# An adaLN attention and Mish block on one core: constants by memset, joint modulation visits, early weight preparation, and another order and pace of the dense work before the first exponential

## The chip, the cores and the metric

The kernel runs on one core of a Trainium2 chip. The metric is the device time of one execution in microseconds; the median of three runs stands for a kernel. Engines: PE is TensorE, DVE VectorE, ACT ScalarE, POOL GpSimd, SP SyncE, which issues every DMA of this kernel.

## The reference

All inputs are float32; x has 2048 rows of 512, there are 32 heads of 16, and F is 1792.

```python
mod = (_silu(c) @ w_mod).reshape(c.shape[0], 6, 1, -1)
sa, ca, ga, sb, cb, gb = (mod[:, i] for i in range(6))
h = _layernorm(x) * (1 + ca) + sa
x = x + ga * (softmax(q @ k.T * Dh ** -0.5) @ v) @ wo      # q, k, v = h @ wqkv
h = _layernorm(x) * (1 + cb) + sb
x = x + gb * (mish(h @ w1 + b1) @ w2)
```

## The kernel before

**Steps.** Attention is cut into 32 iterations n (four blocks of 512 queries by eight groups of four heads). An iteration has 16 steps, one for each 128 keys, and 512 steps t in all, with 20 more (t = -20 to -1) ahead of them. In each step PE makes four products for the softmax maxima of an iteration that lies 20 steps ahead (`max_pair` L493 before t = 0, `max_tile` L479 after it), which DVE reduces (L503, L489); four score products (`score`, L532, L536), whose exponential ACT takes (L539); and the product of older exponentials with the values (`pv`, L554). A step is two half steps; the schedule is written by hand in half steps h = 2t, 2t+1: `at(h, f)` hangs f on a half step, and `run_hooks` runs it there. All instructions of an engine run in the order in which they were emitted, and all DMAs are issued by SP in that order too and share one hardware queue.

**Dense work.** Everything else for PE (the projections to q, k and v, the output projection, the MLP) is cut into units of mostly twelve matmuls of 512 columns, taken in the order of one list when their ready time has come. In steps before t = 0 `whole_units` (L1204) takes as much as a credit allows, `CREDIT` = 7.5 columns blocks of 512 for each step, and the last matmul may run over; a value unit has matmuls of 256 columns, which count one half. From t = 2 on `next_part` (L1185) lays up to eight slots over two steps, one 64-row half in each, beside the score and maximum products. `plan` (L1337) lists the projections: value half 0, keys 1 (`(1, 1)`), queries 1 (`(0, 1)`), keys 2, queries 2, and so on. The end of unit i splits the weights of unit group i+2 into a high and a low part (`slice_split`, ACT and POOL) and loads those of i+3 (`slice_load`). Results go to DRAM scratch, and `load_pair` (L321) brings keys and queries of two heads back into one of NR = 5 buffers `ka`, `qa`. Rows 48 to 63 and 112 to 127 of these hold constants: ones in `ka`, zeros in `qa`, two of them overwritten by minus the maxima (`max_rows` L514, put by four DMAs `qa<-mt`, L525, six half steps ahead of the iteration). The constants come by DMA (`zeros`, `one`, and copies of `ka[0]` for the last three buffers).

**Modulation.** Four vectors of the modulation are made while attention runs: each of eight halves is loaded (`mod_load` L645), summed on POOL, and visited by PE (`mod_unit` L658) as a special between the score products and `pv`; two halves are in flight.

**Preparation.** 32 slices of w1, wo and w2 are then loaded, split on POOL into high and low, and stored to DRAM scratch (`prep_unit` L678, paced by `start_preps` L1392): a new load waits, in half steps, for the store that last used its buffer. `store_at` and `load_at` keep some half steps of an iteration free. When all are stored and the projections done, `open_mlp` gives their space to the MLP, and `first_loads` (L822) loads the first weights of `block(0, 272)`. A block (output projection, transposes, up and down products of one query block) fills 128 steps.

Of the kernel before, what the change touches and what calls it, by code (L numbers as in the profile page):

```python
# [8 lines left out]
F32 = mybir.dt.float32  # L9
F32R = mybir.dt.float32r  # L10
# [8 lines left out]
def adaln_block(ctx: ExitStack, tc: tile.TileContext, x, wqkv, wo, w1, b1, w2, c, w_mod, out):  # L19
# [20 lines left out]
    CUT1, CUT2 = (0, 1), (2, 3)  # L40
    LOV = ((1,), (), (1, 3), (1, 3))
    PREP = 4
    CREDIT = 7.5
    HCAP = 10.0

    x = x[0]
# [77 lines left out]
    def mm(acc, l, r, start, stop):  # L124
        pe_queue.append((acc, l, r, start, stop))
# [71 lines left out]

    def load_at(h):

        return h if h < 60 or 2 <= h % 32 < 20 else h - h % 32 + 28 if 20 <= h % 32 <= 28 else h + -(h - 2) % 32  # L200

    def at(h, f):

# [122 lines left out]
    with ExitStack() as es:  # L326
# [83 lines left out]
        stats_tb(1)  # L410
        tr_tb(0)
        apply_tb(1)
        def zeros(i):
            for b in (48, 112):
                nc.sync.dma_start(qa[i][b:b + 16, :].bitcast(F32), zer[:16, :])

        for i in range(2):
            for b in (48, 112):
                nc.sync.dma_start(ka[i][b:b + 16, :].bitcast(F32), one[:64, :])
            zeros(i)  # L420

        def constants():
            for i in range(2, NR):
                zeros(i)
            for q4 in range(S // TB):
                nc.sync.dma_start(dap(qscr, 48 * S + q4 * TB, [[50 * S, H], [S, 2], [1, TB]]), zer[:64, :])
            nc.sync.dma_start(dap(vscr, VROW - 16, [[VROW, P], [P * VROW, G], [1, 16]]), zer[:, :16 * G])
            nc.sync.dma_start(b1c, b1.rearrange("(f p) -> p f", p=P))
# [226 lines left out]
            mst["row at", i] = h + 7  # L655
        at(h + 7, sums)

    def mod_unit(i):  # L658

        v, o = divmod(i, 2)  # L660
        gate = v in (2, 5)
        acc, row = ring(), mst.pop(("wm", i))[:, 0]
        if gate:
            mm(acc[:, :2 * P], ones.to_broadcast([P, P]), row, True, True)
        else:
            for m in range(2):
                mm(acc[:, m:m + 1], row[:, m * P:(m + 1) * P], ones, True, True)

        def fin(h):
            if gate:  # L670
                nc.scalar.copy(gates[(v - 2) // 3][:, o * 2 * P:(o + 1) * 2 * P], acc[:, :2 * P])
            elif v == 4:
                nc.vector.tensor_scalar_add(modc[:, v - 1, 2 * o:2 * o + 2], acc[:, :2], 1.0)
            else:
                nc.vector.tensor_copy(modc[:, v - 1, 2 * o:2 * o + 2], acc[:, :2])
        return fin

    def prep_unit(h, third, scr, src, gate):  # L678
# [113 lines left out]
    def block(qb, t0):  # L792
# [389 lines left out]
    def queue_special(ready, make):  # L1182
        specials.append((ready, make))
# [146 lines left out]
    def do_specials(h):  # L1330
        if specials and h >= specials[0][0]():
# [27 lines left out]
        return fin  # L1359

    at(-2 * PRO, lambda: slice_load(*plan[2][1:3]))
    order = (4, 5, 10, 11, 6, 7, 8, 9)

    def first_mods(h):
        for i in order[:2]:
            mod_load(i, h)

    def queue_mod(j):
        def make():
            put = mod_unit(order[j])  # L1370

            def fin(h):
                put(h)
                if j + 2 < len(order):
                    mod_load(order[j + 2], h)
                elif j + 1 == len(order):
                    start_preps(h + 2)
            return fin

        queue_special(lambda: mst.get(("row at", order[j]), 4 * T) + 6, make)  # L1380

    for j in range(len(order)):
        queue_mod(j)
    for i, (t0, _, _, args) in enumerate(plan):
        for a in args:
            queue(lambda i=i, t=t0: max(2 * t, split_at.get(i, 4 * T) + 4), lambda tag, i=i, a=a: planned(i, a, tag))

    preps = [(w1scr[f], w1[:, f * P:(f + 1) * P].rearrange("(k p) m -> p k m", p=P), None) for f in range(FT)]
    preps += [(woscr[k], wo[k * P:(k + 1) * P, :], 0) for k in range(DK)]
    preps += [(w2scr[f], w2[f * P:(f + 1) * P, :], 1) for f in range(FT)]  # L1390

    def start_preps(h, i=0, turn=0, puts=()):  # L1392

        if i == len(preps):
            mst["open"] = (max(puts) + 2) // 2
            return
        three = (2, 1, NKC - 1) in put_away
        prep_unit(h, three and turn % 3 == 2, *preps[i])
        puts = (*puts, store_at(h + 9))[-3 if three else -2:]
        then = load_at(max(h + PREP, puts[0] + 1 if len(puts) > 2 - (not three) else 0))  # L1400
        at(then, lambda: start_preps(then, i + 1, turn + 1 if three else 0, puts))

    def prep_step(t):
# [19 lines left out]
    at(2 * (T - 28), lambda: load_ys((0, 1)))  # L1423
    at(2 * (T - 12), lambda: load_ys((2,)))
    at(2 * T - 30, tail_loads)
    for pp in range(2, NR):
        for b in (48, 112):
# [43 lines left out]
```

## Time and profile before

| | before |
|---|---|
| runs | 1700.04, 1703.48, 1704.23 us; median 1703.48 |
| profiled execution | 1704.48 us, its span 1702.7 us, granted clock 0.996 |
| busy | PE 98%, DVE 84%, ACT 80%, POOL 48% of the span |
| DMA | 240.08 MB, 49.5% of 16 engines' span |
| start to the first step (0 to 50.15 us) | layernorm and first projections |
| steps before t = 0 (50.15 to 102.95 us) | maxima of iteration 0 and a part of 1, dense work |
| steps from t = 0 | to about 1600 us |
| last query block's MLP | from there to the end |

Times in the profile count from the span's start. PE's busy time counts overlapping matmuls once and takes in time in which they wait for operands, so a full row does not say that PE does all it can; the pace of the steps, from one `pv` to the next, says more.

### The profile page before, as it was taken

Reading aid. Unit: us, or ns where it says so; the run is one execution under the profiler, and the core shown is the slowest. Engines: PE = TensorE matmul, PEld = TensorE weight load, DVE = VectorE, ACT = ScalarE, POOL = GpSimd, SP = SyncE. Lnnn points to the kernel's source line nnn. Section 1 sums busy time; section 2 is a strip of 40 time slices with the busy share of each in tenths; the row PEclk is TensorE's granted clock in tenths of the full one; section 3 lists DMA queues with packets and bytes.
Section 4 is the critical chain, followed back from the end, with each engine's and each line's share of the span. In section 5 each row is a group of like instructions: output and inputs, shape, how many; then the busy total and the mean of one; then the engine's idle time right before and its main releaser. Section 6 shows DMA issues by size and latency. Waiting matters only on the chain.

```text
span 1702.7 us, 33730 instructions
## 1 busy us (share of the span) xinstructions
PE 1674.4 (98%) x12406; PEld 921.7 (54%) x12406; DVE 1438.2 (84%) x2372; ACT 1359.4 (80%) x2614; POOL 809.3 (48%) x829
## 2 busy tenths in 40 slices
PE   7999999999999999999999999999999999999999
PEld 5755665455444545555555455555555455555587
DVE  6888888888889898888889898888889888884377
ACT  6257777777778998888888998888888988888674
POOL 5155224565513465645433464655323564555442
PEclk9999999999999999999999999999999999999999
DMA  7777467777773343425364434435354433433261
GB/s 252 186 233 216 111 163 214 238 229 217 236 219 94 89 105 90 128 78 135 80 161 122 129 73 109 124 76 139 78 141 134 130 93 76 142 105 127 78 229 62
DMA packets 113997, 240.08 MB, mean 141 GB/s; under 512 B 24048, under 2 KB 49648, under 8 KB 107784
## 3 DMA queue, kind: packets, MB, share of 16 engines
q1 hardware_dynamic: 113832, 237.92, 49.5%
q8 instruction: 98, 1.61, 0.4%
q14 instruction: 67, 0.55, 0.1%
HBM read 179.95 MB, written 51.44 MB: 136 GB/s over the span
## 4 chain that ended last, share of the span: by engine, by line
PE 90%; DVE 3%; DMA 3%; ACT 2%; issue 1%; SPq 0%; POOL 0%; ACTq 0%; DVEq 0%; POOLq 0%
PE bk L554 28%; PE ring L536 22%; PE ring L487 19%; PE bk L136 10%; PE bk L129 3%; PE ring L1162 2%; PE ring L129 2%; DVE mx L489 2%; ACT pr L539 1%; DMA qa<-mt 1%; DMA xt<-in_A_x 1%; PE ring L501 1%; DMA w<-w1scr 1%; DMA w<-woscr 1%; PE ring L865 0%
## 5 line engine op out<-in xcount | busy, mean ns | idle before, releaser
L489 DVE TENSOR_REDUCE mx<-ring 128x1 f32<-128x512 f32 x1968 | 1222.9, 682 | 159.5 <-PE ring L487 138.0
L539 ACT ACTIVATE pr<-ring 128x512 f32<-128x512 f32 x2048 | 1079.0, 602 | 216.2 <-PE bk L136 118.0
L487 PE MATMUL ring<-ka,qa 64*128 64x512 f32 x1968 | 819.0, 429 | 3.0 <-DMA od<-ot 1.3
L536 PE MATMUL ring<-qa,ka 64*128 64x512 f32 x2048 | 761.3, 403 | 6.8 <-DMA qa<-mt 4.0
L554 PE MATMUL bk<-pr,vg 128*32 128x512 f32 x4096 | 546.8, 606 | 0.0
L487 PEld LDWEIGHTS ring<-ka,qa 64*128 64x128 f32 x1968 | 350.8, 184 | 331.6 <-DVE mx L489 248.1
L536 PEld LDWEIGHTS ring<-qa,ka 64*128 64x128 f32 x2048 | 374.1, 184 | 201.5 <-DVE mx L489 114.0
L136 PE MATMUL bk<-h,w 64*128 64x512 f32 (+1 forms) x1080 | 279.0, 391 | 0.0
L136 PE MATMUL bk<-w,a_h 64*128 64x512 f32 x632 | 210.6, 413 | 0.0
L136 PEld LDWEIGHTS bk<-h,w 64*128 64x128 f32 x1080 | 178.3, 184 | 9.6 <-ACT pr L539 1.5
L554 PEld LDWEIGHTS bk<-pr,vg 128*32 128x32 f32 x4096 | 80.8, 108 | 136.9 <-issue 127.8
L136 PE MATMUL bk<-w,a_l 64*128 64x512 f32 x316 | 124.2, 393 | 0.0
L136 PEld LDWEIGHTS bk<-w,a_h 64*128 64x128 f32 x632 | 106.9, 184 | 2.6
L921 POOL TENSOR_TENSOR y<-yd,y 128x512 f32<-128x512 f32 x44 | 56.9, 1293 | 89.5 <-ACT yd L920 84.6
L756 POOL TENSOR_SCALAR qq<-ee 128x512 f32<-128x512 f32 x25 | 15.5, 622 | 169.1 <-ACT ee L750 169.1
L772 POOL TENSOR_TENSOR qq<-qq,rr 128x512 f32<-128x512 f32 x42 | 54.2, 1291 | 83.6 <-ACT rr L766 83.4
L758 POOL TENSOR_TENSOR hb<-hb,ee 128x512 f32<-128x512 f32 x42 | 54.1, 1289 | 82.4 <-DVE ee L754 80.4
L136 PE MATMUL bk<-w,o_hl 64*128 64x512 f32 x288 | 79.8, 407 | 0.0
L98 POOL TENSOR_TENSOR a_l<-hb,a_h 128x512 fp32r<-128x512 f32 x53 | 72.2, 1363 | 4.4
L136 PEld LDWEIGHTS bk<-w,a_l 64*128 64x128 f32 x316 | 58.3, 184 | 2.3
L136 PE MATMUL bk<-h_h,wl 64*128 64x512 f32 x168 | 57.5, 423 | 0.0
L774 POOL TENSOR_TENSOR rr<-rr,qq 128x512 f32<-128x512 f32 x42 | 54.1, 1289 | 3.5
(206 smaller groups left out, 1857.9 us busy)
## 6 DMA issues: line engine op xcount, KB each, us to landing
ka<-kscr SPq DMA_DIRECT2D x124, 384.0 KB
w<-w2scr SPq DMA_DIRECT2D x56, 512.0 KB
w<-w1scr SPq DMA_DIRECT2D x46, 512.0 KB
vg<-vscr SPq DMA_DIRECT2D x32, 552.0 KB
qa<-qscr SPq DMA_DIRECT2D x124, 100.0 KB
kscr<-qh SPq DMA_DIRECT2D x16, 512.0 KB
qscr<-qh SPq DMA_DIRECT2D x32, 256.0 KB
hl<-in_B_w SPq DMA_DIRECT2D x28, 256.0 KB
```

The costliest lines, as they stand in the source:

```text
L98: (nc.gpsimd if eng == "p" else nc.vector).tensor_sub(lo, src, hi.bitcast(F32))
L129: nc.tensor.matmul(acc, l, r, start=start, stop=stop)
L136: i = nc.tensor.matmul(acc, l[64 * g:64 * g + 64], r[64 * g:64 * g + 64], start=start and not then, stop=bool(stop and then))
L487: nc.tensor.matmul(pm, qt[64 * s:64 * s + 64, qs * P:(qs + 1) * P], kt[64 * s:64 * s + 64, kb * TB:(kb + 1) * TB], start=True, stop=True)
L489: nc.vector.tensor_reduce(out=mxs[n][:, s, 4 * j + qs, kb:kb + 1], in_=pm, op=ALU.max, axis=AX.X)
L536: nc.tensor.matmul(p_, kt[64 * s:64 * s + 64, kc * P:(kc + 1) * P], qt[64 * s:64 * s + 64, :], start=True, stop=True)
L539: e = nc.scalar.activation(pr, p_, AF.Exp, scale=SCALE)
L554: nc.tensor.matmul(accs[n][32 * h:32 * h + 32, :], vgs[n][:, o:o + 32], pts.pop((t, h)), start=(kc == 0), stop=(kc == 15))
L758: (nc.vector if tail else nc.gpsimd).tensor_mul(hb, hb, ee)
L772: nc.gpsimd.tensor_mul(qq, qq, rr)
L774: nc.gpsimd.tensor_mul(rr, rr, qq)
L921: nc.gpsimd.tensor_add(y[i], yd, y[i])
```

## The change

It has these parts, in the order of the code:

- `CREDIT` is 7.4, and `whole_units` keeps in `cur["owed"]` what a step took too much or too little.
- The constant rows of `qa` and `ka` come from POOL memsets of whole tiles, three of 128x2048 for `ka[2:]` after the setup; 20 small DMAs go.
- In `plan` queries 1 stand ahead of keys 1, so their weights are loaded and split in the setup; units before t = 0 are ready two half steps after their split, not four.
- `mod_unit` visits both halves of a vector at once, four visits, one vector in flight.
- Six w1 slices are prepared early (`early_prep`), from h = -34 on, every three half steps, in the buffers of the exponentials; `start_preps` does the other 26. Its waits are one half step longer, and loads begin at h % 32 = 4 instead of 2.
- `first_loads` leaves the two w1 tiles and three w2 tiles to half steps 279 to 287.
- `load_pair(2n)` for n = 3, 4, 5, 7 stands at half step 2 of iteration n-2, not at 9 or 15.

```diff
-    CREDIT = 7.5
+    CREDIT = 7.4
-        return h if h < 60 or 2 <= h % 32 < 20 else ... else h + -(h - 2) % 32
+        return h if h < 60 or 4 <= h % 32 < 20 else ... else h + -(h - 4) % 32
...
-        slice_load(1, 1, pw)
+        slice_load(0, 1, pw)
-        one = lp.tile([P, TB], F32, name="one")
-        nc.gpsimd.memset(one, 1.0)
+        for i in range(NR):
+            nc.gpsimd.memset(qa[i].bitcast(F32), 0.0)
+        for i in range(2):
+            nc.gpsimd.memset(ka[i].bitcast(F32), 1.0)
...
-        for i in range(2):
-            for b in (48, 112):
-                nc.sync.dma_start(ka[i][b:b + 16, :].bitcast(F32), one[:64, :])
-            zeros(i)
         def constants():
-            for i in range(2, NR):
-                zeros(i)
...
-        slice_split(1, 1)
+        slice_split(0, 1)
     ka += [kq2.tile([P, S], F32R, name=f"ka{i}") for i in range(2, NR)]
+    for t in ka[2:]:
+        nc.gpsimd.memset(t.bitcast(F32), 1.0)
...
-    def mod_unit(i):
-        v, o = divmod(i, 2)
+    def mod_unit(v):
         gate = v in (2, 5)
-        acc, row = ring(), mst.pop(("wm", i))[:, 0]
-        if gate:
-            mm(acc[:, :2 * P], ones.to_broadcast([P, P]), row, True, True)
-        else:
-            for m in range(2):
-                mm(acc[:, m:m + 1], row[:, m * P:(m + 1) * P], ones, True, True)
+        acc, rows = ring(), [mst.pop(("wm", 2 * v + o))[:, 0] for o in range(2)]
+        for o, row in enumerate(rows):
+            if gate:
+                mm(acc[:, o * 2 * P:(o + 1) * 2 * P], ones.to_broadcast([P, P]), row, True, True)
+            else:
+                for m in range(2):
+                    mm(acc[:, 2 * o + m:2 * o + m + 1], row[:, m * P:(m + 1) * P], ones, True, True)
...
         def first_loads(h):
             mst["w2 at"] = 0
-            more_w2(h + 1, NA)
+            more_w2(h + 1, DK)
             load(h + 2, y, lambda i: load_y(qb, i), range(4))
-            load(h + 9, w1s, load_w1, range(2))
+            load(t0 + 7, w1s, load_w1, range(2))
+            at(t0 + 10, lambda: more_w2(t0 + 11, NA - DK))
...
     def whole_units(h, credit):
-        while credit > 0:
+        cur["owed"] = cur.get("owed", 0) + credit
+        while cur["owed"] > 0.49:
             if not cur["left"]:
                 if not units or h < units[0][0]():
+                    cur["owed"] = 0
                     return
...
-            credit -= m[0].shape[-1] / TB
+            cur["owed"] -= m[0].shape[-1] / TB
...
-    plan = [(-PRO, 2, 0, range(4, 16)), (-PRO, 1, 1, range(NB)), (-PRO, 0, 1, (0,)), (-PRO, 1, 2, range(NB)),
+    plan = [(-PRO, 2, 0, range(4, 16)), (-PRO, 0, 1, (0,)), (-PRO, 1, 1, range(NB)), (-PRO, 1, 2, range(NB)),
...
-    order = (4, 5, 10, 11, 6, 7, 8, 9)
-    def first_mods(h):
-        for i in order[:2]:
-            mod_load(i, h)
+    order = (2, 5, 3, 4)
+    def first_mods(h, j=0):
+        for o in range(2):
+            mod_load(2 * order[j] + o, h + 2 * o)
...
-            queue(lambda i=i, t=t0: max(2 * t, split_at.get(i, 4 * T) + 4), ...)
+            queue(lambda i=i, t=t0: max(2 * t, split_at.get(i, 4 * T) + (2 if t < 0 else 4)), ...)
...
+    EARLY = 6
+    def early_prep(i, h):
+        scr, src, _ = preps[i]
+        lo, hi = [ap.tile([P, TB], F32R, tag=f"p{(1, 3, 0, 2)[i % 4]}", name="ep", bufs=4 - i % 4 // 2) for _ in range(2)]
+        raw = lo.bitcast(F32)
+        nc.sync.dma_start(raw.rearrange("p (k m) -> p k m", m=P), src)
+        def split():
+            hi_copy("p", hi, raw)
+            lo_sub("p", lo, raw, hi)
+        def put():
+            for v, part in enumerate((hi, lo)):
+                nc.sync.dma_start(scr[:, v, :], part.bitcast(F32))
+        at(h + 7, split)
+        at(h + 10, put)
+    for i in range(EARLY):
+        at(3 * i - 34, lambda i=i: early_prep(i, 3 * i - 34))
-    def start_preps(h, i=0, turn=0, puts=()):
+    def start_preps(h, i=EARLY, turn=0, puts=()):
...
-        then = load_at(max(h + PREP, puts[0] + 1 if ...))
+        then = load_at(max(h + PREP, puts[0] + 2 if ...))
...
-            at(32 * (n - 2) + (15 if n % 2 == 0 else 9), lambda n=n: load_pair(2 * n))
+            at(32 * (n - 2) + (2 if n in (3, 4, 5, 7) else 15 if n % 2 == 0 else 9), lambda n=n: load_pair(2 * n))
...
-    for pp in range(2, NR):
-        for b in (48, 112):
-            nc.sync.dma_start(ka[pp][b:b + 16, :].bitcast(F32), ka[0][b:b + 16, :].bitcast(F32))
```

More of the change, by code (lines that the diff above doesn't have):

```diff
@@ L198, in load_at @@
     def load_at(h):
[L200 removed]
+        return h if h < 60 or 4 <= h % 32 < 20 else h - h % 32 + 28 if 20 <= h % 32 <= 28 else h + -(h - 4) % 32
     def at(h, f):
@@ L656, in mod_load @@
         at(h + 7, sums)
-    def mod_unit(i):
-        v, o = divmod(i, 2)
+    def mod_unit(v):
         gate = v in (2, 5)
-        acc, row = ring(), mst.pop(("wm", i))[:, 0]
-        if gate:
-            mm(acc[:, :2 * P], ones.to_broadcast([P, P]), row, True, True)
-        else:
-            for m in range(2):
-                mm(acc[:, m:m + 1], row[:, m * P:(m + 1) * P], ones, True, True)
+        acc, rows = ring(), [mst.pop(("wm", 2 * v + o))[:, 0] for o in range(2)]
[5 more added lines that the diff above has]
+                    mm(acc[:, 2 * o + m:2 * o + m + 1], row[:, m * P:(m + 1) * P], ones, True, True)
         def fin(h):
             if gate:
-                nc.scalar.copy(gates[(v - 2) // 3][:, o * 2 * P:(o + 1) * 2 * P], acc[:, :2 * P])
+                nc.scalar.copy(gates[(v - 2) // 3], acc)
             elif v == 4:
-                nc.vector.tensor_scalar_add(modc[:, v - 1, 2 * o:2 * o + 2], acc[:, :2], 1.0)
+                nc.vector.tensor_scalar_add(modc[:, v - 1, :], acc[:, :DK], 1.0)
             else:
-                nc.vector.tensor_copy(modc[:, v - 1, 2 * o:2 * o + 2], acc[:, :2])
+                nc.vector.tensor_copy(modc[:, v - 1, :], acc[:, :DK])
         return fin
@@ L1373, in fin @@
                 put(h)
-                if j + 2 < len(order):
-                    mod_load(order[j + 2], h)
-                elif j + 1 == len(order):
+                if j + 1 < len(order):
+                    first_mods(h, j + 1)
+                else:
                     start_preps(h + 2)
             return fin
-        queue_special(lambda: mst.get(("row at", order[j]), 4 * T) + 6, make)
+        queue_special(lambda: mst.get(("row at", 2 * order[j] + 1), 4 * T) + 6, make)
     for j in range(len(order)):
@@ L1385, in adaln_block @@
         for a in args:
-            queue(lambda i=i, t=t0: max(2 * t, split_at.get(i, 4 * T) + 4), lambda tag, i=i, a=a: planned(i, a, tag))
+            queue(lambda i=i, t=t0: max(2 * t, split_at.get(i, 4 * T) + (2 if t < 0 else 4)), lambda tag, i=i, a=a: planned(i, a, tag))
     preps = [(w1scr[f], w1[:, f * P:(f + 1) * P].rearrange("(k p) m -> p k m", p=P), None) for f in range(FT)]
@@ L1399, in start_preps @@
         puts = (*puts, store_at(h + 9))[-3 if three else -2:]
-        then = load_at(max(h + PREP, puts[0] + 1 if len(puts) > 2 - (not three) else 0))
+        then = load_at(max(h + PREP, puts[0] + 2 if len(puts) > 2 - (not three) else 0))
         at(then, lambda: start_preps(then, i + 1, turn + 1 if three else 0, puts))
@@ L1425, in adaln_block @@
     at(2 * T - 30, tail_loads)
-    for pp in range(2, NR):
-        for b in (48, 112):
-            nc.sync.dma_start(ka[pp][b:b + 16, :].bitcast(F32), ka[0][b:b + 16, :].bitcast(F32))
     for pp, h in ((2, -22), (3, -8)):
```

2 lines of the change are left out of this document (removed).

## The prediction

> **What bounds the kernel now.** I read the page first: its span, the engines' shares and the chain that ended last.
>
> ```profile
> span 1702.7 us, 33730 instructions
> PE 1674.4 (98%) x12406; PEld 921.7 (54%) x12406; DVE 1438.2 (84%) x2372; ACT 1359.4 (80%) x2614; POOL 809.3 (48%) x829
> PE 90%; DVE 3%; DMA 3%; ACT 2%; issue 1%; SPq 0%; POOL 0%; ACTq 0%; DVEq 0%; POOLq 0%
> ```
>
> PE carries the chain. The profiled execution took 1704.48 us, 1.8 more than its span and 1.0 more than the median of the runs (1703.48); I sum against 1704.48 and take 1.0 off at the end. PE does the same matmuls after the change (the joint visits too), so only lost time can go: DMA waits in the chain, switches at the modulation visits, and unevenness ahead of step 0. The timeline of PE gives the pace, by the starts of `pv`.
>
> ```profile
> 180.28 1.06 PE L554 MATMUL bk<-pr,vg 128*32 128x512 f32 x8
> 183.13 1.07 PE L554 MATMUL bk<-pr,vg 128*32 128x512 f32 x8
> 186.60 1.07 PE L554 MATMUL bk<-pr,vg 128*32 128x512 f32 x8
> ...
> 122.08 1.06 PE L554 MATMUL bk<-pr,vg 128*32 128x512 f32 x8
> 125.64 0.64 PE L554 MATMUL bk<-pr,vg 128*32 128x512 f32 x4
> ```
>
> A plain step takes 2.85 us (180.28 to 183.13). One with a visit takes 3.47 (a vector in columns) or 3.56 (a gate, from 122.08). Three places lie far off this pace:
>
> ```profile
> 337.27 1.06 PE L554 MATMUL bk<-pr,vg 128*32 128x512 f32 x8
> 340.32 0.46 PE L536 MATMUL ring<-qa,ka 64*128 64x512 f32 x1 [1.98 <-DMA qa<-mt]
> 342.76 1.93 PE L554 MATMUL bk<-pr,vg 128*32 128x512 f32 x8
> 346.57 0.64 PE L554 MATMUL bk<-pr,vg 128*32 128x512 f32 x4
> ...
> 433.01 1.06 PE L554 MATMUL bk<-pr,vg 128*32 128x512 f32 x8
> 435.84 0.46 PE L536 MATMUL ring<-qa,ka 64*128 64x512 f32 x1 [1.76 <-DMA qa<-mt]
> 437.66 1.07 PE L554 MATMUL bk<-pr,vg 128*32 128x512 f32 x8
> ...
> 490.74 1.06 PE L554 MATMUL bk<-pr,vg 128*32 128x512 f32 x8
> 494.03 0.46 PE L487 MATMUL ring<-ka,qa 64*128 64x512 f32 x1 [1.26 <-DMA od<-ot]
> 496.12 1.94 PE L554 MATMUL bk<-pr,vg 128*32 128x512 f32 x8
> 500.04 1.06 PE L554 MATMUL bk<-pr,vg 128*32 128x512 f32 x8
> ```
>
> The first: steps of 5.49 and 3.81, 3.6 us above two plain ones. The second: 4.65, 1.8 above. The third: 5.38 and 3.92, 3.6 above. Two wait for the maxima's rows; the third I read as a wait for the keys of pair 19, queued beside the `od` rows that the profile names.
>
> **The stall in iteration 4 (-3.5) and in 6 (-1.8).** SP's timeline shows why the rows came late.
>
> ```profile
> 320.13 0.50 SPq L689 DMA_DIRECT2D w1scr<-hl  x1
> 327.86 0.33 SPq L682 DMA_DIRECT2D hl<-in_A_wo  x1
> 332.85 2.76 SPq L525 DMA_DIRECT2D qa<-mt  x4
> ...
> 479.80 0.43 SPq L695 DMA_DIRECT2D w<-w1scr  x1
> 481.12 0.80 SPq L319 DMA_DIRECT2D ka<-kscr  x2
> ```
>
> From 320.6 to 327.9 SP stands still before the load of slice 16 (h = 146): its buffer's last store was issued at h = 143 behind pair 12 in the queue. Everything after it slid, the value load, a query store and the rows of h = 154. In the new plan that phase is: query store and slice store at 141, pair 12 at 143, the load that needs this store at 144. Pair 12 now queues behind the store, so SP stands about 1 us instead of 7.3, and the rows go out on time, six half steps (8.6 us) ahead of need. In iteration 6 the same: the store at 205, pair 16 at 207 behind it, the load at 208. What is late next is PE's own pace. Cover gone, each costs what it costs now. Pairs 6, 8, 10 and 14 move to half step 2, past the sums and rows of half steps 4 and 5, which then queue behind two pairs. The tightest is h = 36: pair 5, two modulation loads, pair 6 and a query store stand ahead, some 3.8 MB; DVE's reciprocal waits at h = 46, 14.3 us later, with the maxima behind it, and PE behind these. At 289 GB/s (row below) that is 13.2 us: nothing, or 2 us if the queue is late. I book +0.7 for this and other new waits.
>
> **The stall in iteration 8 (-3.6).** The load of pair 19 (481.12) stood behind two w1 and two w2 tiles, a third w2 tile right after it, 512 KB each. All five move to h = 279 to 287, so pair 19's load (h = 256) finds 2.1 MB less before it, 7 us at the rate below, against a wait of 1.3 us that with its consequences cost 3.6. w1 is first needed after the transposes (h = 300), 19 half steps after its load. Pair 21 (h = 288) then stands behind the same tiles, but is needed only at h = 296, 24 us after the first of them: with the value load ahead 4.2 MB, 14.5 us at 289 GB/s. Bound: 0 to -4.
>
> The clock belongs to these terms:
>
> ```profile
> 340.00:343.00 3.00, 2.68 (x18) 1.82 (x22) 2.14 (x4) 1.78 (x4) 2.05 (x2) 0.72 0.71 165
> 494.00:497.00 3.00, 2.97 (x20) 1.56 (x20) 2.09 (x4) 1.77 (x3) 0.00 (x0) 0.66 0.04 12
> ```
>
> After the pauses the granted clock was 0.72 and 0.66, and the next step cost 1 us more; I count that step in. The Trainium skill ("TensorE: Matmul & The Clock Gate", The HAM clock gate) has the clock halved only after an idle window of about 3.4 us. By that rule the two second steps would not go with the stalls, and the sum would be 2 us less; the trace, with a pause of 1.98 us and a clock of 0.72, does not agree.
>
> **Modulation (-0.9).** Eight visits cost 0.62 (columns) or 0.71 (gate) above 2.85. A joint visit switches PE's tiling once and does the work twice. Bounds: from four whole visits saved (4 x 0.66, -2.7) to nothing; a visit is mostly its matmuls, so I take a third, 4 x 0.23.
>
> **Early preparation and opening (0 after step 0).** Six slices fewer follow, but four vectors at one in flight end at h = 64, not 58, and the longer waits slow the rest: by the plan's arithmetic the last store falls at h = 241, before at 239; the MLP opens one step later; the first unit of block 0 starts at step 128 both times. The queue of dense work from step 0 on is the same unit for unit, as are the gaps without any.
>
> **Ahead of step 0 (+1.1).**
>
> ```profile
> 50.15 0.73 PE L501 MATMUL ring<-ka,qa 64*128 64x512 f32 x4
> 71.36 0.73 PE L501 MATMUL ring<-ka,qa 64*128 64x512 f32 x4
> 74.01 0.73 PE L501 MATMUL ring<-ka,qa 64*128 64x512 f32 x4
> 79.34 0.73 PE L501 MATMUL ring<-ka,qa 64*128 64x512 f32 x4
> 80.34 1.09 PE L129 MATMUL bk<-h_h,wh 128*128 128x512 f32 x4
> 82.05 0.73 PE L501 MATMUL ring<-ka,qa 64*128 64x512 f32 x4
> 102.95 0.47 PE L536 MATMUL ring<-qa,ka 64*128 64x512 f32 x1 [0.27 <-DMA qa<-mt]
> ...
> 60.00:75.00 15.00, 15.00 (x108) 12.00 (x108) 13.23 (x12) 2.62 (x7) 0.00 (x0) 1.00 0.57 107
> 75.00:80.00 5.00, 5.00 (x28) 3.26 (x26) 4.39 (x5) 0.99 (x2) 0.17 (x1) 1.00 1.03 222
> 80.00:100.00 20.00, 19.78 (x90) 12.51 (x88) 18.45 (x19) 3.61 (x7) 10.00 (x10) 1.00 1.01 289
> ...
> 79.83 1.29 POOL L98 TENSOR_TENSOR wl<-wr,wh 128x512 fp32r<-128x512 f32 x1 [27.05 <-ACT wh L91]
> 94.73 0.62 POOL L95 TENSOR_SCALAR qh<-qf 128x512 fp32r<-128x512 f32 x1 [0.71 <-ACT qf L259]
> ...
> 99.53 3.02 SPq L525 DMA_DIRECT2D qa<-mt  x4
> ...
> L503 DVE TENSOR_REDUCE mx<-ring 128x2 f32<-128x1024 f32 x40 | 46.8, 1220 | 4.1 <-PE ring L501 4.0
> ```
>
> The 20 steps took 52.8 us: 2.65 with 7.5 blocks of values, 2.71 with eight blocks of keys, and near the end one step with a single block, where queries 1 were done and keys 2 not ready. Both plans do 148 blocks here. At 7.4 in every step and 0.27 a block (a quarter of 1.09) the sum is 10 x 2.62 + 10 x 2.55 = 51.7: PE is ready at 101.9, 1.1 earlier; DVE's reductions are no bound (46.8 us in the same steps).
>
> The DMA queue is not. Shares times lengths make 33.9 us of queue work from 60 to 100. Six early slices add 4.7 MB (by their shapes 256 KB in and 512 KB out each; all sizes here go by shapes), 16.3 us at 289 GB/s. Off go twelve small constants (0.98 MB, 3.4 us) and one key store that now follows the rows (0.79 MB, 2.7 us). That leaves 44.1, so the rows of iteration 0, planned for h = -6 behind early stores, key stores and pair 3, land near 104.1 (they were issued at 99.53 and, PE's row says, in time to 0.27 us). PE waits 2 us for them: +1.1. Bounds: -1.1 if the queue keeps up; +9.8 if it works as from 60 to 75, 107 GB/s at share 0.57, 188 at a full one: the slices then take 25 us and the rows land at 112.7. I stand near the 289, the row nearest to the rows' own time. By the Trainium skill ("DMA: Bandwidth & Descriptors", Where 436 GB/s comes from) the memory gives a core about 358 GB/s; by that estimate the slices take 13.1 us, the rows land at 100.9, and PE does not wait. No long row here reaches it.
>
> POOL idled 27 us before 79.83; there go three memsets and the first three early splits at 0.62 + 1.29 each. The low part of keys 1, now needed early in step -9 instead of far later, stands behind them: 0 to +1.5, kept in the range. An early store waits for POOL's split and holds SP, with load_pair(2) and value stores behind it, needed no earlier than step -4.
>
> **Sum.** +1.1 - 0.9 - 3.5 - 1.8 - 3.6 + 0.7 = -8.0: 1696.5 for a profiled execution, 1695.5 as a median.
>
> **The rivals.** (a) The queue keeps up ahead of step 0: -1.1 instead of +1.1, so 1693.3. For it: 60 to 75 ran at share 0.57. Against: 80 to 100 was full. (b) Iterations 4 and 6 stay late: the queue, not SP's standing still, delays the rows, or the earlier pairs bring the wait elsewhere. Then 5.3 are missing: 1700.8, no change. For it: even from their issue the rows took 7.5 us to reach PE (332.85 to 340.32). (c) Slower: the queue in front of the first maxima's rows works at 188 GB/s, because the early loads come in short rows. The rows land at 112.7, 8.7 later than in the forecast, and as the queue is then the bound, 4 and 6 stay late too: -8.0 + 8.7 + 5.3 = +6.0, 1709.5. It decides from a landing at about 112 on. (d) The change does not even out the steps: 1.1 less gain for PE, hidden under the rows' landing: 1695.5 as well.
>
> **Numbers.** What measurement can tell here is about 0.3%, 5.1 us: faster is below 1698.4, slower above 1708.6. Forecast with (d) 0.45, (a) 0.20, (b) 0.20, (c) 0.15. So 0.65, 0.20 and 0.15. The likeliest case alone spans 1693 to 1698. The range, 1690 to 1705, goes down by rival (a) and the deeper bounds of the visits and of iteration 8, up through (b) and a late low part of keys 1.
>
> **What would show it.** Right: steps near 2.85 at iterations 4, 6 and 8 without low-clock windows; four steps near 3.9 instead of eight near 3.5; even steps near 2.6 before step 0, whose first score product waits for `qa<-mt` at about 104; DMA share near 1.0 from 70 on. Wrong: that product later than 107 or before 102, stalls over 1 us on `qa<-mt` or `ka<-kscr` between 200 and 500, or a gap of dense work of another length around 443 to 487.

## The result, and the profile after

| | before | after |
|---|---|---|
| median of 15 runs each | 1702.76 us (1698.58 to 1704.89) | 1705.89 us (1704.12 to 1708.05) |
| ratio | | 1.0023, 95% interval 1.0017 to 1.003 |
| profiled execution, its span | 1704.48 us, 1702.7 us | 1705.29 us, 1703.5 us |

The change costs 0.2%: less than the 0.3% that the prediction counted as a difference, but above its range. The page of the changed kernel hardly differs:

```profile
span 1703.5 us, 33729 instructions
PE 1673.5 (98%) x12406; PEld 923.7 (54%) x12406; DVE 1443.3 (85%) x2370; ACT 1358.1 (80%) x2612; POOL 820.1 (48%) x838
```

Equal totals hide two large opposite terms. PE's timeline shows the first, the stalls that went (starts of `pv`, now L547; score products are L529, the maxima's rows L518):

```profile
131.72 1.07 PE L547 MATMUL bk<-pr,vg 128*32 128x512 f32 x8
135.71 1.06 PE L547 MATMUL bk<-pr,vg 128*32 128x512 f32 x8
...
346.51 1.06 PE L547 MATMUL bk<-pr,vg 128*32 128x512 f32 x8
349.35 1.06 PE L547 MATMUL bk<-pr,vg 128*32 128x512 f32 x8
...
439.00 1.06 PE L547 MATMUL bk<-pr,vg 128*32 128x512 f32 x8
441.96 1.07 PE L547 MATMUL bk<-pr,vg 128*32 128x512 f32 x8
...
495.13 1.06 PE L547 MATMUL bk<-pr,vg 128*32 128x512 f32 x8
497.98 1.06 PE L547 MATMUL bk<-pr,vg 128*32 128x512 f32 x8
```

The steps that took 5.49, 4.65 and 5.38 us now take 2.84, 2.96 and 2.85; a joint visit takes 3.99. From the first `pv` of an iteration to that of the next, iteration 4 went from 49.64 to 46.07 us, 6 from 47.89 to 46.22, 8 from 50.74 to 46.99, and 0 and 1 together from 97.85 to 96.73.

The second term lies ahead of step 0. The waits of PE there, and the first `pv`:

```profile
90.41 0.97 PE L129 MATMUL bk<-h_h,wh 128*128 128x512 f32 x3 [1.40 <-ACT qf L259]
101.82 0.80 PE L129 MATMUL bk<-h_h,wh 128*128 128x512 f32 x1 [2.76 <-ACT qf L259]
112.54 0.47 PE L529 MATMUL ring<-qa,ka 64*128 64x512 f32 x1 [2.23 <-DMA qa<-mt]
120.06 1.06 PE L547 MATMUL bk<-pr,vg 128*32 128x512 f32 x8
```

The first score product comes at 112.54 instead of 102.95, the first `pv` at 120.06 instead of 109.69: 10.4 us, which eat all of the 10.1 won later. (The two profiled spans differ by only 0.8 us and the medians by 3.1, since the profiled execution of the kernel before lies 1.7 us above its median and that of the changed one 0.6 below its own.) In the windows (columns: PE, PEld, DVE, ACT and POOL busy, granted clock, DMA share, GB/s) the queue is not even full where the loss begins, 0.76 against 1.01 in the kernel before:

```profile
60.00:75.00 15.00, 15.00 (x108) 12.00 (x108) 13.35 (x13) 2.76 (x8) 8.46 (x7) 1.00 0.96 248
80.00:100.00 20.00, 17.55 (x76) 10.73 (x76) 16.78 (x17) 2.54 (x5) 10.35 (x12) 1.00 0.76 237
100.00:112.00 12.00, 8.49 (x24) 5.00 (x24) 4.71 (x4) 1.69 (x3) 3.30 (x4) 0.72 0.91 284
```

ACT, POOL, SP's issues and the chain of waits say why:

```profile
89.25 0.62 ACT L91 CAST wh<-wr 128x512 fp32r<-128x512 f32 x1 [7.71 <-DMA wr<-in_A_wqkv]
...
113.76 0.59 ACT L259 COPY qf<-bk 128x512 f32<-128x512 f32 x1 [7.43 <-POOL ql L98]
```

```profile
89.94 1.28 POOL L98 TENSOR_TENSOR wl<-wr,wh 128x512 fp32r<-128x512 f32 x1 [4.38 <-ACT wh L91]
...
111.75 0.62 POOL L95 TENSOR_SCALAR qh<-qf 128x512 fp32r<-128x512 f32 x1 [6.56 <-DMA kscr<-qh]
```

```profile
83.68 0.80 SPq L1403 DMA_DIRECT2D w1scr<-ep  x2
91.25 0.38 SPq L231 DMA_DIRECT2D wr<-in_A_wqkv  x1
```

```profile
81.91 7.32 DMA wr<-in_A_wqkv
...
97.56 5.50 DMA kscr<-qh
...
104.50 7.91 DMA qa<-mt
```

The load of the weights of keys 2 took 7.3 us in the crowded queue. ACT stood for it in the split, with the copy of a finished block behind it; PE waited for that copy's bank, and POOL for ACT. SP stood for POOL: after the store that it began at 83.68 it issued nothing until 91.25, when POOL had made the low part of these weights and the next load could take their place. Then the same happened once more. The key store issued at 97.56 took 5.5 us, POOL stood for it with the next keys until 103.21, and SP's next key stores stood for POOL, with the maxima's rows right behind them. So the rows were issued at 104.50, not at 99.53, and then took 7.9 us more (3.3 in the kernel before). Meanwhile POOL waited for another key store to free a buffer, ACT for POOL, and the first exponential stood behind ACT's copy at 113.76.

### The profile page after: what moved, and what is told of

The parts are those of the page before. It is cut to its first block, busy times and chain, and to the rows that moved or that the text cites. A ratio compares the mean times of both kernels' runs of the same rounds, so it can differ in the third digit from the quotient of the medians.

```text
span 1703.5 us, 33729 instructions
## 1 busy us (share of the span) xinstructions
PE 1673.5 (98%) x12406; PEld 923.7 (54%) x12406; DVE 1443.3 (85%) x2370; ACT 1358.1 (80%) x2612; POOL 820.1 (48%) x838
## 4 chain that ended last, share of the span: by engine, by line
PE 89%; DMA 3%; DVE 3%; ACT 2%; POOL 1%; issue 1%; SPq 1%; ACTq 0%; POOLq 0%; DVEq 0%
PE bk L547 29%; PE ring L529 22%; PE ring L480 20%; PE bk L136 10%; PE ring L1156 2%; PE bk L129 2%; PE ring L129 2%; DVE mx L482 2%; ACT pr L532 1%; DMA qa<-mt 1%; DMA xt<-in_A_x 1%; PE ring L859 0%; DMA wr<-in_A_wqkv 0%; PE ring L509 0%; DVE hf L392 0%
## 5 line engine op out<-in xcount | busy, mean ns | idle before, releaser
L529 PE MATMUL ring<-qa,ka 64*128 64x512 f32 x2048 | 760.7, 403 | 6.6 <-ACT pr L532 3.5
L547 PE MATMUL bk<-pr,vg 128*32 128x512 f32 x4096 | 545.1, 604 | 0.0
L529 PEld LDWEIGHTS ring<-qa,ka 64*128 64x128 f32 x2048 | 374.2, 184 | 200.5 <-DVE mx L482 114.1
L547 PEld LDWEIGHTS bk<-pr,vg 128*32 128x32 f32 x4096 | 80.8, 108 | 136.2 <-issue 126.7
L95 POOL TENSOR_SCALAR qh<-qf 128x512 fp32r<-128x512 f32 x27 | 16.8, 623 | 88.3 <-ACT qf L259 61.4
```

What stands on the lines that cost most here:

```text
L529: nc.tensor.matmul(p_, kt[64 * s:64 * s + 64, kc * P:(kc + 1) * P], qt[64 * s:64 * s + 64, :], start=True, stop=True)
L547: nc.tensor.matmul(accs[n][32 * h:32 * h + 32, :], vgs[n][:, o:o + 32], pts.pop((t, h)), start=(kc == 0), stop=(kc == 15))
```

## The experiments

One number collects whatever is shifted among the waits: the start of iteration 2, that is its first `pv`. The table is read from each profile; "E" is the number of early slices.

| kernel | E | first score product | first `pv` | iteration 0 | iteration 1 | iteration 2 starts |
|---|---|---|---|---|---|---|
| before | 0 | 102.95 | 109.69 | 49.22 | 48.63 | 207.54 |
| after | 6 | 112.54 | 120.06 | 48.50 | 48.23 | 216.79 |
| e1 no early slices | 0 | 103.15 | 112.06 | 48.63 | 48.35 | 209.05 |
| e2 old order | 6 | 107.86 | 114.38 | 48.56 | 48.25 | 211.19 |
| e3 late split | 6 | 106.19 | 114.24 | 48.54 | 48.26 | 211.04 |
| f11 the same, timed | 6 | 108.15 | 116.77 | 48.51 | 48.25 | 213.53 |
| e4 slices alone | 6 | 116.27 | 123.00 | 49.24 | 48.62 | 220.87 |
| f4 loads alone | 6 | 111.44 | 118.19 | 49.79 | 48.25 | 216.23 |
| f1 pair 3 later | 6 | 103.10 | 113.55 | 51.07 | 48.25 | 212.88 |
| f2 copy later | 6 | 102.68 | 113.02 | 50.95 | 48.22 | 212.19 |
| f3 values first | 6 | 103.37 | 110.12 | 53.17 | 48.24 | 211.54 |
| f5 visit later | 6 | 103.21 | 109.96 | 50.16 | 51.76 | 211.89 |
| f6 rows earlier | 6 | 103.42 | 110.18 | 53.23 | 48.24 | 211.65 |
| f7 five slices | 5 | 102.44 | 109.19 | 53.37 | 48.23 | 210.79 |
| f9 slices sooner | 6 | 104.99 | 111.74 | 53.95 | 48.27 | 213.97 |
| f8 no slices | 0 | 102.41 | 109.17 | 48.86 | 48.35 | 206.38 |
| f10 one row sooner | 6 | 102.78 | 109.53 | 50.47 | 48.25 | 208.26 |

e3 and f11 are one kernel: from execution to execution this stage varies by 2.5 us. Two more runs below, g and h, do ahead of iteration 1 what the changed kernel does, and start iteration 2 at 217.67 and 219.57 instead of 216.79. So smaller differences between single profiles decide nothing.

**First question: volume or order?** Theory A: the slices' 4.7 MB fill the queue. Theory B: queries 1 ahead of keys 1 leave too little time between the load of keys 2's weights and their split, where ACT then stands.

```diff
# e1 (and first_loads not before the later opening)
-    EARLY = 6
+    EARLY = 0
```

> The changed kernel without the six early slices (all 32 are prepared after the modulation, so block 0 of the MLP opens some 18 steps later; read only the time of the first score product, 102.95 us before and 112.54 us after the change). Theory A, volume: the early slices' 4.7 MB fill the DMA queue and everything late comes from that; the first score product then stands at 102 to 103 us, with no pause of PE over 0.5 us ahead of it. Theory B, order: queries 1 ahead of keys 1 leaves three half steps between the load of the weights of keys 2 and their split, ACT stands at that split until they land, and the copies of results behind it hold PE; without the early slices the load still takes some us, so PE still pauses 1 us or more and the product stands at 104 to 107 us.

First product at 103.15, close to A's 102 to 103, and no pause at the weights. The whole took 1730.15 us, as the MLP opens later. But the first `pv` came at 112.06, not 109.7: the first exponential still stood behind ACT's copy, and that behind POOL, with the queue only 0.64 busy in the stretch before.

```profile
75.00:100.00 25.00, 24.88 (x119) 16.01 (x116) 23.20 (x23) 5.23 (x10) 10.16 (x10) 1.00 0.64 163
```

```profile
105.03 0.59 ACT L259 COPY qf<-bk 128x512 f32<-128x512 f32 x1 [6.01 <-POOL ql L98]
```

```diff
# e2: the old order and pace of the dense work, the slices kept
# (besides, the old CREDIT, whole_units and first weights of the setup)
-    plan = [(-PRO, 2, 0, range(4, 16)), (-PRO, 0, 1, (0,)), (-PRO, 1, 1, range(NB)), ...
+    plan = [(-PRO, 2, 0, range(4, 16)), (-PRO, 1, 1, range(NB)), (-PRO, 0, 1, (0,)), ...
```

> The changed kernel with the order of before (keys 1, queries 1, keys 2) and its pace (7.5 blocks, nothing carried over) ahead of step 0, and with the early slices. Theory A (volume): the queue is as full as with the change, the maxima's rows land late, the first score product stands at 109 us or later. Theory B (order): ACT has seven steps between load and split, does not stand, and the product is back at 103 to 105 us.

1698.8 us, and 107.86: between the two theories. (This time, that of e3 and that of e4 are single runs; the kernel before took 1699.40 us beside them.)

```diff
# e3: when unit 1 (queries 1) ends, split the weights of keys 2 six half steps later
-                    d = 4 if h > 0 else 1
+                    d = 4 if h > 0 else 7 if i == 1 else 1
-                    at(h + (7 if h > 0 else 2), lambda: slice_load(...))
+                    at(h + (7 if h > 0 else 8 if i == 1 else 2), lambda: slice_load(...))
```

> The changed kernel with one thing moved: the split of the weights of keys 2 stands six half steps later (h = -9 instead of -15), and the load behind it (queries 2) with it. The bytes are the same. Theory A (volume): the first score product stays at 110 us or later, since the queue in front of the maxima's rows is as long. Theory B (order): ACT no longer stands 7.7 us at the split, the pauses of PE at 88 and at 99 us go, and the product stands at 103 to 106 us.

1699.68 us, first product at 106.19. The rows went out at 99.69, 4.8 us sooner, and PE no longer paused earlier. So ACT's stand was a cause; but the rows still took until 106.19, and POOL still waited for a key store. The landing at 106.19 lies just past B's 103 to 106.

```profile
106.19 0.76 PE L529 MATMUL ring<-qa,ka 64*128 64x512 f32 x1 [2.91 <-DMA qa<-mt]
```

**e4**: the kernel before, with `early_prep` of six slices and nothing else of the change.

> The kernel before with the six early slices alone added (26 are left for later, so the MLP opens earlier as well). Theory A (volume): the first score product moves from 102.95 to 108 us or later. Theory B (order): it stays within 2 us, 103 to 105 us.

1711.76 us, first product at 116.27: B, as stated, fell. In the old order too the slices make ACT, POOL and SP stand for each other:

```profile
91.63 0.58 ACT L259 COPY qf<-bk 128x512 f32<-128x512 f32 x1 [10.10 <-POOL ql L98]
...
104.57 0.58 ACT L259 COPY qf<-bk 128x512 f32<-128x512 f32 x1 [8.47 <-POOL ql L98]
```

A surprise beside it: iterations 4, 6 and 8 took 47.03, 46.11 and 46.64 us here, with the old places of all loads (iteration 5 lost 1.4). And e1, with no early slice, had taken 46.11 in both 4 and 6.

**Second: what took the later stalls away?** g undoes the moves of pairs 6, 8, 10 and 14, h those of the first MLP loads.

```diff
# g
-        at(32 * (n - 2) + (2 if n in (3, 4, 5, 7) else 15 if n % 2 == 0 else 9), ...)
+        at(32 * (n - 2) + (15 if n % 2 == 0 else 9), ...)
# h
-            more_w2(h + 1, DK)
+            more_w2(h + 1, NA)
-            load(t0 + 7, w1s, load_w1, range(2))
-            at(t0 + 10, lambda: more_w2(t0 + 11, NA - DK))
+            load(h + 9, w1s, load_w1, range(2))
```

> Changed kernel with the loads of pairs 6, 8, 10 and 14 back at half steps 15 and 9. Theory P (these moves took the stalls away): iteration 4 back to 49 to 50 us and iteration 6 to 47.5 to 48, 4.5 to 5.3 us longer in all. Rival O (the earlier opening, and the slice loads that it shifts, took them away, as with the six early slices alone on the kernel before, where iterations 4 and 6 took 47.0 and 46.1): iteration 4 at 46 to 47.2, iteration 6 at 46.0 to 46.4, 0 to 1.2 us longer in all.

> Changed kernel with the first loads of the MLP back where they were (all third w2 tiles and both w1 tiles up to 9 half steps behind the opening). Theory P (moving them took the stall of iteration 8 away): iteration 8 back to 49.5 to 51 us, 2.5 to 4 us longer in all. Rival O (the shifted opening did): iteration 8 at 46.5 to 47.2, within 0.5 us.

g: iterations 4 and 6 at 46.11 and 46.08, as in the changed kernel; only iteration 5 lost, 47.17 against 46.39, by a wait of 1.07 us on `qa<-mt`. h: iteration 8 at 47.39, 0.40 more, with this left of the stall:

```profile
503.22 0.49 PE L529 MATMUL ring<-qa,ka 64*128 64x512 f32 x1 [0.30 <-DVE mx L482]
```

Both moves thus brought about 1.2 us together. (1706.59 and 1707.67 us, single runs.) In iterations 4 and 6 the gain came with the shifted phase of the slices: the six early ones shift it without the longer waits (e4), and the longer waits without the early ones (e1, which keeps the moved pairs). No run moves the phase alone.

In iteration 8 what h keeps of the change is the opening one step later. SP's timelines show what stands between the maxima's rows and the load of pair 19 (512 KB a weight tile, 256 KB a tile of `y`): 2.4 MB before, 2.1 in h, 1.6 in e4, 1.0 after. The iteration took 50.74, 47.39, 46.64 and 46.99 us. One more run, f7 below, opens two steps later still: three wo tiles and three of `y`, again 2.4 MB, stand there, PE waits 1.02 us for the keys, and the iteration takes 49.68, though all five tiles are moved. This points to the time of the opening, more than to the five tiles, as what decides how much stands ahead of pair 19; no run moves the opening alone.

**Third: take the waits ahead of step 0 away one by one.**

```diff
# f1: both weight splits later, pair 3 behind the rows
+                    d = 4 if h > 0 else {1: 7, 2: 12}.get(i, 1)
+                    at(h + (7 if h > 0 else {1: 8, 2: 13}.get(i, 2)), lambda: slice_load(...))
-    for pp, h in ((2, -22), (3, -8)):
+    for pp, h in ((2, -22), (3, -5)):
# f2: besides, the copy of the first block of keys 2 from half step 0 to 2
+            if (i, a) == (3, 0):
+                at(h + 2, lambda: unit(h + 2))
```

> Changed kernel with three places moved: the split of the weights of keys 2 from half step -15 to -9, the split of the weights of queries 2 from -3 to 8 (each with the weight load behind it), and pair 3 from half step -8 to -5, behind the first maxima's rows on SP. All six early slices stay. Theory A (volume: the early slices' 4.7 MB fill the queue, so the rows land late wherever they stand): first score product at 106 or later, pv(0) at 114 or later, as with the late split alone (106.19, 114.2). Theory B (order: what stands ahead in the in-order queues sets the time): rows issued 3 to 4 us sooner, first score product at 102 to 104, pv(0) at 110 to 112.5; time 1695 to 1698.

> As the run with pair 3 later, and the copy of the results of the first block of keys 2 moved from half step 0 to 2, behind the first exponentials on ACT. Theory A: rows land late, so ACT has time anyway: pv(0) as in the run with pair 3 later, within 0.3 us. Theory B, with its second hold (ACT waits in this copy for POOL, POOL for the landing of a key store, 2.8 to 7.4 us in the runs so far, and the first exponentials stand behind it): pv(0) 1 to 3 us sooner than in that run, and the first exponential within 1.5 us of the first score product.

First products at 103.10 and 102.68, with no wait: order does bring the rows in time, with all six slices in the queue, and in f2 the first exponential followed at 103.21 instead of 104.62. But the first `pv` came only at 113.55 and 113.02 (1701.79 and 1700.94 us): the values of iteration 0 now stood behind pair 3. So theory B held for the first product, and neither theory for the first `pv`. f2:

```profile
113.02 1.94 PE L547 MATMUL bk<-pr,vg 128*32 128x512 f32 x8 [3.51 <-DMA vg<-vscr]
```

```profile
112.00:115.00 3.00, 1.98 (x10) 0.31 (x10) 0.00 (x0) 0.00 (x0) 1.13 (x1) 0.50 1.06 377
115.00:118.00 3.00, 3.00 (x14) 2.35 (x16) 1.96 (x3) 1.28 (x3) 1.56 (x1) 0.50 1.07 382
118.00:122.00 4.00, 4.00 (x34) 1.62 (x30) 2.81 (x6) 3.93 (x8) 3.76 (x5) 0.98 0.12 44
```

After the pause the clock was 0.50, and the step took 5.41 us instead of 3.05.

```diff
# f3: f2 with the values of iteration 0 at half step -5, pair 3 at -3
# f4: the changed kernel with these two moves alone (pair 3 from -8)
-    at(-3, lambda: load_v(0))
+    at(-5, lambda: load_v(0))
-    for pp, h in ((2, -22), (3, -5)):
+    for pp, h in ((2, -22), (3, -3)):
```

> As the run with the copy later, with the loads behind the first maxima's rows in another order: the values of iteration 0 at half step -5 instead of -3, pair 3 at -3 instead of -5, so that the 1.2 us of pair 3's issues and its 1.6 MB stand behind the values. Theory B (order): the pause of 3.5 us on the values and the slow first step behind it (5.41 us, granted clock 0.50) go, pv(0) at 109.2 to 110.5, iteration 0 at 48.4 to 48.8, 5.5 to 6.5 us less than the run with the copy later: 1694 to 1696, a ratio to the kernel before of 0.996 to 0.9975. Theory A (volume): another transfer of the full queue takes the place of the one moved, pv(0) at 112 or later, time 1698 or more.

> Changed kernel with only the two loads moved (values of iteration 0 to half step -5, pair 3 to -3); all splits and copies as in the changed kernel. If the order on SP alone was the cause, the first score product comes at 102 to 104 and pv(0) at or below 111. If ACT's stand at the weights of keys 2 (7.7 us in the changed kernel) is a cause of its own, PE still pauses over 1 us twice ahead of step 0, the rows go out about 2 us sooner than in the changed kernel, the first score product comes at 107 to 110, and pv(0) at 113 to 117.

f3: first `pv` at 110.12, within the expected 109.2 to 110.5, and yet 1701.37 us, ratio 0.9991 (0.998 to 1.0002). A third transfer was late, as theory A had it: the first modulation rows, with POOL's sums behind them; that step took 7.06 us and the next 4.35:

```profile
128.32 0.70 PE L129 MATMUL ring<-wm,ones 128*128 128x256 f32 x2 [2.80 <-POOL wm L647]
```

f4, 1706.10 us: with ACT standing at the weights PE paused 1.48 and 2.67 us as in the changed kernel, and moving the loads gave 1.1 us (111.44), less than expected. The split is the first thing to mend.

f5 lets the first visit wait two half steps (`+ (8 if j == 0 else 6)` in `queue_special`); f6 loads both first rows at half step -4, ahead of key stores and pair 3, and keeps the step of the visit (`+ 10`).

> As the run with the values first, with the first joint modulation visit two half steps later, so that POOL's sums, 2.8 us late there (step of 7.06 us and the next of 4.35), are ready when PE comes. Theory B (order: each wait removed ahead of step 0 only showed the next one in the chain, and this was the last): no pause on the sums, pv(0) still at 109.2 to 110.5, iteration 0 at 48.4 to 49.0, span 1693.5 to 1694.8 with a ratio to the kernel before of 0.9955 to 0.9975. Theory A (volume: the traffic in front of step 0 costs its time somewhere in iteration 0 or 1, wherever it is put): iteration 0 stays above 51 us or iteration 1 takes over the loss, ratio 0.998 or more.

> As the run with the values first, with the first modulation vector's loads (1 MB) at half step -4, ahead of two key stores and pair 3, and the first visit at the same step as there. Theory B: no pause on the sums either; the two key stores land about 3.5 us later (1 MB at 290 GB/s), so POOL's wait for them (4.76 us there) grows and may hold ACT's copy in step 3 by up to 3 us; iteration 0 at 48.4 to 51.5, pv(0) as there within 0.5 us. Theory A: iteration 0 above 52 us.

f5: 1701.15 us, ratio 1.0002 (0.9989 to 1.0015). Iteration 0 fell to 50.16, but the visits, now two half steps later, met late sums in iteration 1: 51.76. f6: 1700.23 us; the rows were in time, and the keys of pair 3 late instead, with a step of 6.78 us. Both came out as theory A said, the loss only changing its place:

```profile
116.64 0.47 PE L480 MATMUL ring<-ka,qa 64*128 64x512 f32 x1 [1.92 <-DMA ka<-kscr]
```

**Fourth: is that a floor set by the volume?** Seven orders (e2, e3, f1, f2, f3, f5, f6) had brought iteration 2 to between 211 and 213.5 us. f8 is f3 without early slices, f7 with five, f9 with the six four half steps sooner.

> As the run with the values first, but none of the six slices prepared early (all 36 after the modulation rows, so the MLP opens some 18 steps later and the whole is longer; only the time up to the start of iteration 2 counts). Theory V (volume: the queue has more to move than it can before iteration 1, and the lack shows at whichever transfer stands last): no pause over 1 us in iterations 0 and 1, which take 48.5 and 48.3, and iteration 2 starts at 206.3 to 207.8, 4 us sooner than with the slices. Theory O (order alone: the last waits come from where loads stand): the pause at the modulation sums stays, iteration 0 above 51, iteration 2 at 210.5 or later.

> As the run with the values first, with five early slices instead of six: 0.79 MB less ahead of step 0, 2.7 us of queue time at 290 GB/s; the MLP opens two steps later. Theory V: the loss of 4.6 us at the first modulation visit shrinks to 0 to 3, iteration 2 starts at 208.5 to 210.8. Theory O: as with six, 211 to 212.

> As the run with the values first, with all six early slices two steps (5.3 us) sooner. In its stretch of 60 to 66 us the queue's share is 0.70 to 0.75, so 1.6 us of queue time is free there. Theory V: iteration 2 starts 1 to 2 us sooner, at 209.5 to 210.5. Theory O: as there, 211 to 212, or later if POOL's memsets hold the splits and SP with them.

f8 starts iteration 2 at 206.38, as theory V said, with no long wait and a half-empty queue; its 1726.83 us again count the late opening:

```profile
75.00:100.00 25.00, 24.88 (x118) 15.87 (x116) 23.33 (x23) 4.61 (x9) 10.69 (x11) 1.00 0.50 150
```

f7 gained 0.75 us at most, and the loss at the first visit did not shrink (4.8 us against 4.6). Its time, 1703.22, also holds the longer iteration 8 told above and 1.4 us more in iteration 5. f9 was later, at 213.97 (1702.21 us). Neither shows a slope, but both lie within the scatter of one kernel, so the form of the dependence stays open.

```diff
# f10: f3 with the first of the two modulation rows ahead of pair 3 and two key stores,
#      and the weights of queries 2 split eight half steps later still
-                at(max(0, h + 2), lambda: first_mods(max(0, h + 2)))
+                at(-4, lambda: mod_load(2 * order[0], -4))
+                at(0, lambda: mod_load(2 * order[0] + 1, 2))
```

> As the run with the values first, with the first of the two loads of the first modulation vector (0.5 MB) ahead of two key stores and pair 3, its sums on POOL ahead of the next keys' splits, and the split of the weights of queries 2 eight half steps later, off POOL's way (1.3 us). If the loss is one late load in front of an in-order engine: the second sums end near 121 to 126, before PE's visit at 125.5, pause under 0.5 us, iteration 0 at 48.5 to 49.5, iteration 2 at 207 to 208.5, span 1693.5 to 1696, ratio to the kernel before 0.9955 to 0.9985. If the queue's volume is a floor: pair 3 or the key stores become the late transfer, iteration 2 at 210.5 or later, ratio 0.998 to 1.001.

> The kernel of the run with the late split, timed: changed kernel with only the split of the weights of keys 2 six half steps later. Its profile lost 4.5 us against the kernel before up to iteration 0 and won 9.0 in iterations 4, 6 and 8 and 1.0 at the modulation; by the sum it should be 4 to 5 us below the kernel before and 5 to 6 below the changed one: 1696 to 1699, ratio 0.997 to 0.9985. If the gains later shift with the start, as the changed kernel's did not: ratio 0.999 or more.

f10: **1696.87 us, ratio to the kernel before 0.9971 (0.996 to 0.9981)**, below both kernels, though 0.9 us above the 1693.5 to 1696 expected. Iteration 2 starts at 208.26, the upper edge of what was expected, with iteration 0 at 50.47 against the 48.5 to 49.5 expected; the sums are no longer late, and pair 3's keys still are a little, with a step of 4.85 us:

```profile
115.89 0.46 PE L480 MATMUL ring<-ka,qa 64*128 64x512 f32 x1 [0.70 <-DMA ka<-kscr]
```

f11: 1701.43 us, ratio 0.9994 (0.9985 to 1.0003): the late split alone only returns to the kernel before. The 4 to 5 us expected of it were read off one favourable profile.

So both theories were half of it. In the changed order the slices cost 7.7 us (216.79 against 209.05 without them), in f3's order 5.2 (211.54 against 206.38), and the best order found with slices, f10, stays 1.9 behind f3's without them (208.26 against 206.38). Without slices, order is worth 2.7 (209.05 against 206.38), with them 8.5; all to within the scatter of single profiles. The volume makes single transfers slow, 5.5 to 7.9 us from issue to landing in the rows shown; which wait that becomes, and how many engines it stops in turn, is the order's doing.

## Why the prediction was wrong, step by step

**Ahead of step 0 (+1.1): the step that failed**, mis-sized at +10.4. Three parts of it:
- *The rows' landing, "near 104.1".* It was a sum of bytes over one rate, which lets SP issue on plan. SP issued them 5.0 us late (104.50 for 99.53), and the product came 8.0 us behind the issue, not 3.4. The chain of engines that stand for each other, from a weight load to ACT to POOL to SP and again from a key store to POOL to SP, was not in the sum. The prediction saw that a store "holds SP" behind POOL's split, but not that POOL itself stood behind ACT, and ACT behind a weight load.
- *PE "ready at 101.9", 1.1 earlier.* Where PE waited for nothing (f1, f2, f3, f5 to f8, f10), its first product came at 102.4 to 103.4, against 102.95 before. The evening out of steps did bring something: in f10 the first step begins at 50.59, so the 20 steps took 52.2 us, as in f1 and f8, against 52.8 before (0.27 of it a wait) and 51.7 by the sum. That is 0.3 to 0.6 us of the 1.1. It doesn't show in the time of the first product, because the first step itself began between 50.2 and 51.1 in these runs, against 50.15. Rival (d) was half right.
- *What follows the rows.* The first exponential came 1.71 us behind the first product, at 114.25, and 0.51 behind it before; up to the first `pv` that left 0.8 us more (112.54 to 120.06 is 7.52, before 6.74).

**Iteration 4 (-3.5), 6 (-1.8): right**, measured -3.57 and -1.67. The reason given, the phase of the slice stores, is what g leaves standing, and e4 and e1 each shift it by another part of the change; the moved pairs, which the prediction did not credit, brought 0.8 in iteration 5.

**Iteration 8 (-3.6): right in size (-3.75), by luck in part.** That what stands ahead of pair 19 sets the stall agrees with the five runs above, but moving the five tiles brought only 0.40 (h). The rest goes with the opening one step later, which the prediction mentioned and priced at nothing; f7 shows that the stall returns with the tiles moved.

**Modulation (-0.9): right**, -1.12. **Other new waits (+0.7): right in size**: about +0.9 in iterations 5, 11 and 15 (0.3 each). The place worked out for it, h = 36 in iteration 1, shows no wait (48.23 us). **Opening (0): right**; the dense gap in iteration 7 is unchanged, 44.48 and 44.55.

With 10.4 in place of 1.1 and the other measured terms the sum is +1.2; the profiled spans differ by 0.8.

Of the rivals, (a) fell with the landing and (b) with iterations 4 and 6. Rival (c) named the landing almost to the digit, 112.7 against 112.4, but not for its reason: from 100 to 112 the queue moved 284 GB/s, not 188, and its other half, 4 and 6 staying late, did not come. A landing forecast by a rate was met by a late issue. By the estimate drawn from the Trainium skill ("DMA: Bandwidth & Descriptors", Where 436 GB/s comes from) the rows would have landed at 100.9; the trace, with 112.4, does not agree.

## What to carry to other kernels

A transfer's price in a crowded stage is its time from issue to landing, here 5.5 to 7.9 us, and each in-order engine that meets it early passes the wait on to all that stands behind: follow every early transfer to the instruction that waits for it, and what is queued there, before adding up bytes. Judge a mend by a point behind the whole stage, not by the wait it removes: f1, f2, f3 and f6 each took a wait away, and that point stayed within 1.4 us until f10. And put loads into a full queue in the order of need, splits and copies behind what is urgent; that alone turned 0.2% lost into 0.3% won.

## What the runs showed of the hardware

The granted clock has a level of 0.50 that pauses of a few us can bring: 0.50 in the windows from 112 to 118 us, after the pause of 3.51 us that ended at 113.02 (f2). In the changed kernel shorter ones did it as well:

```profile
91.00:94.00 3.00, 3.00 (x15) 1.73 (x15) 2.15 (x2) 0.59 (x1) 2.83 (x5) 1.00 0.42 109
...
103.00:106.00 3.00, 3.00 (x10) 1.87 (x9) 2.36 (x2) 0.78 (x2) 1.90 (x2) 0.50 0.70 183
...
112.00:115.00 3.00, 1.06 (x8) 0.66 (x8) 1.89 (x3) 1.24 (x3) 2.92 (x4) 1.00 0.86 293
115.00:118.00 3.00, 3.00 (x13) 2.05 (x15) 2.33 (x4) 3.00 (x7) 1.82 (x2) 0.51 0.51 131
```

After the pause of 1.40 us that ended at 90.41 it stayed at 1.00, and after the one of 2.76 at 101.82 it was 0.50. After the one of 2.23 at 112.54 it was still 1.00; only behind a second one, 1.40 us up to 114.90, it was 0.51. The length of a pause alone does not settle it: 2.03 us in e1, up to 106.16, left 0.99, and 1.98 us in the kernel before, up to 340.32, gave 0.72. The Trainium skill ("TensorE: Matmul & The Clock Gate", The HAM clock gate) knows a full and a half clock, the half one after an idle window of about 3.4 us: the two levels agree, the length does not, with 0.50 after 2.76 us. The slow clock made the pause in f2 cost 1.7 times its length: 3.51 us, and 2.4 in the step behind it.
